# Two chained feed-forward layers behind a scan: the first two blocks of the first layer interleaved, with the weights loaded to match

## Chip, core and metric

One core of one Trainium2 chip. The metric is the device time of one execution in microseconds; the kernel before takes 623.9 us (median of three runs, 623.71 to 626.47).

## What is computed

A state-space scan over 4 sequences of 768 tokens (8 heads, 32 values and 16 states per head, chunks of 32 tokens), then two dense layers over the 3072 tokens, each 256 to 2048 to 256:

```python
for c in range(nc):                       # 24 chunks of 32 tokens
    M = CB * L                            # decayed C B^T inside the chunk
    y[:, :, sl] = einsum(M, xc) + einsum(Cc, state) * exp(cum)
    state = decay_full * state + sum(Bx)  # carried to the next chunk
x = attn_out.transpose(0, 2, 1, 3).reshape(B * S, H * D)
x = leaky_relu(x @ moe_w_in, 0.01) @ moe_w_out
return relu(x @ moe2_w_in) ** 2 @ moe2_w_out
```

## The kernel before

The tokens are cut into 12 **pieces** of 256. A piece is scanned in two halves. `scan_a` (lines 336 to 379) makes the scaled fp16 operands, the decays and the product S; `scan_b` (381 to 423) carries the states, forms Y on TensorE in two steps (lines 397 to 399, then 418 and 419) and ends with `yh` on ScalarE and `yl` on VectorE (lines 422 and 423). `yh` and `yl` are the input of the first layer, as a high and a low part; `yl` comes last, and no product of a block starts before it. From the second piece on, fp16 operands that are spread out over heads (`kbd`, `xbh`, `xbl`, `sbd`) are written by four DMAs each on the SP queue (line 332).

The first layer runs in **blocks**: six of one piece, then three of two. A block has 16 slices of the 2048 hidden values. In a one-piece block a step takes two slices: 12 matmuls for the hidden values (`hmm`, lines 443 to 445, into one of three PSUM buffers `hp`), two ScalarE instructions and one VectorE instruction that split the activation into `g` (lines 466 to 468), and, two steps later, 12 matmuls into the block's output `oo` (`omm`, lines 485, 486 and 491). So a block of one piece has 8 steps, 96 hidden matmuls and 96 output matmuls.

The weights lie in memory as 64-bit pairs. One **chunk** (512 KB) serves one step's hidden matmuls (`1i`) or output matmuls (`1o`). It is loaded by SP into one of seven staging buffers (`wst`), and takes three ScalarE (lines 126, 129, 161) and three VectorE instructions (137, 139, 162) to become two fp32r parts. The queue `wq` (line 105) holds all 8 chunks of `1i`, then all 8 of `1o`, then the second layer's. `w_step` works one chunk of each phase on; it is called once per step while chunks of the first layer remain.

The order of the program is fixed by the loop over blocks at line 643. `stages_to(due(...))` (lines 612 and 625) says how far the scans have come at each step; within a stage, `scan_b` of one piece and `scan_a` of the next are drawn in turn (line 601), except in stage 1, where `scan_b` runs first (line 597). Each engine takes its instructions in the order it was given, which a scheduler derives from the program's order and the dependencies. The second layer (`Two`, lines 509 to 582) follows when all blocks are done.

Of the kernel before, what the change touches and what calls it, by code (L numbers as in the profile page):

```python
# [24 lines left out]
NP = BATCH * NPC  # L25
# [5 lines left out]
KI, KO = DM // P, FF // P  # L31
# [6 lines left out]
LAG = {1: 2, 2: 3}  # L38
# [2 lines left out]
RATE = 1.4 / KO  # L41
LEAD = 4
NSTEP = 15
NHEAP = 24


# [5 lines left out]
def ssd_moe_kernel(ctx: ExitStack, tc: tile.TileContext, in1, in2, w1i, w1o, w2i, w2o, out):  # L52
# [10 lines left out]
    sm = ctx.enter_context(tc.tile_pool(name="sm", bufs=2))  # L63
    heap = ctx.enter_context(tc.tile_pool(name="heap", bufs=NHEAP))
    ap_ = ctx.enter_context(tc.tile_pool(name="ap", bufs=2))
# [5 lines left out]
    def big(shape, dtype, name, tag="b", bufs=None):  # L71
        return heap.tile(shape, dtype, tag=tag, name=name, bufs=bufs)
# [29 lines left out]
        return t[:, 0], t[:, 1]  # L102


    wq = [(nm, c) for nm in ("1i", "1o", "2i", "2o") for c in range(8)]
    w_loaded, w_half, w_full = [], [], []

    def load_w():
# [83 lines left out]
    def load_piece(p):  # L192
        v = sp.tile([P, U * (N + T + D)], F32, tag="in1", name="in1", bufs=2)
        w = sp.tile([P, U * 2 * T], F32, tag="in2", name="in2", bufs=2)
        nc.sync.dma_start(v, in1[p])
        nc.sync.dma_start(w, in2[p])
        return part(v, N + T, D), part(v, 0, N), part(w, T, T), part(v, N, T), part(w, 0, T), part(w, 0, T + N)
# [89 lines left out]
    def sequence_scales(s):  # L287

        mx = sm.tile([P, 5], F32, tag="mx", name="mx")
        all_ = in1[NPC * s : NPC * s + NPC].rearrange("a p f -> p a f")  # L290

        for to, at in ((0, N + T), (3, N + T + 16), (1, N), (4, N + 16), (2, 0)):
            t = big([P, NPC, U * 16], F32, "all", "st", 7)
            nc.sync.dma_start(t, all_[:, :, U * at : U * (at + 16)])
            yield
            squares(mx[:, to : to + 1], t)
            yield
        sc, isc, sbp = yield from powers(mx, 5)

        fac = sm.tile([P, 1], F32, tag="fac", name="fac")  # L300
        nc.vector.tensor_tensor(fac, isc[:, 0:1], isc[:, 2:3], ALU.mult)
        nc.vector.scalar_tensor_tensor(fac, fac, 1.0 / KK, isc[:, 1:2], ALU.mult, ALU.mult)
        for p in range(NPC * s, NPC * s + NPC):
            scales[p] = sc[:, 0:1], sc[:, 2:3], sc[:, 1:2], sbp, fac, KK, 1.0
# [121 lines left out]
    blocks, q0 = [], 0  # L426
# [75 lines left out]
    def split_y(g):  # L502
        y = yf.pop(g)
        h, l = (big([P, 2, KI, TP], F32R, t, "y", 4) for t in ("xh", "xl"))
        nc.scalar.copy(h, y)
        nc.vector.tensor_tensor(l, y, h.bitcast(F32), ALU.subtract)
        ys[g] = h, l
# [77 lines left out]
    def piece_y(p):  # L585
        return lambda: tuple(t[:, p % 2] for t in y_of(p))
# [6 lines left out]
    def stage(k):  # L593
        a = scan_a(k, loaded.pop(k)) if k < NP else iter(())
        b = scan_b(k - 1, piece_y(k - 1)) if k > 0 else iter(())
        bd = sequence_scales(k // NPC + 1) if k % NPC == NPC - 1 and k + 1 < NP else iter(())
        if k == 1:
            yield from b
        n = 0
        live = [b, a, bd]  # L600
        while live:
            live = [g for g in live if next(g, g) is not g]
            n += 1
            if n == 4 and k + 1 < NP:
                loaded[k + 1] = load_piece(k + 1)
            yield

    sc_it = (k for k in range(NP + 1) for _ in stage(k))
    now = [0, 0]
    cum = []  # L610

    def stages_to(x):
        while now[0] < NP + 1 and now[0] + min(now[1] / NSTEP, 0.99) < x:
            k = next(sc_it, NP + 1)
            now[:] = (k, now[1] + 1) if k == now[0] else (k, 0)

    stages_to(1)
    stages_to(1 + 13.5 / NSTEP)
    for _ in range(8):
        w_step()  # L620


    starts = [(KO * p0 - LEAD, p0 + n + 1) for p0, n in blocks[1:]]

    def due(at):
        return max(nb - max(RATE * (b - at), 0) for b, nb in starts)

    pend = []

    def second(lag):  # L630
        while len(pend) > lag:
            ph_, ms, end = pend.pop(0)
            ph_.omm(ms)
            if end:
                ph_.finish()

    def need(nm, m):
        while (nm, m) not in w_done:
            (w_step if nm[0] == "1" else w_one)()

    pos = 0
    acc = 0.0
    for i, (p0, n) in enumerate(blocks):
        ph_ = One(p0, n)
        for m in range(0, KO, 2 // n):
            ms = list(range(m, m + 2 // n))
            need("1i", m // 2)
            ph_.hmm(ms)
            pos += 2
            ph_.act(ms)  # L650
            stages_to(due(pos + 2))
            pend.append((ph_, ms, ms[-1] == KO - 1))
            if len(pend) > LAG[n]:
                need("1o", pend[0][1][-1] // 2)
            second(LAG[n])
            first_w = wq[:1] and wq[0][0][0] == "1" or any(v[0][0] == "1" for v in w_loaded + w_half + w_full)
            acc += 1.0 if first_w else (0.3 if i < len(blocks) - 1 else 1.5)
            while acc >= 1:
                acc -= 1
                (w_step if first_w else w_one)()  # L660
            if i == len(blocks) - 1 and m == KO - 4:
                split_y(0)
        if p0 % 2 + n == 2:
            ys.pop(p0 // 2)
    second(0)

    for g in range(NG):
        ph_ = Two(g)
# [64 lines left out]
```

## Time and profile before

| | |
|---|---|
| median of three runs | 623.9 us |
| profiled execution, its own time | 623.66 us |
| its span, first to last instruction | 621.9 us (1.76 us lie around it) |
| TensorE busy | 574.2 us (92%) |
| VectorE busy | 462.8 us (74%) |
| ScalarE busy | 450.8 us (72%) |

TensorE is busy in nine tenths or more of every slice of the span from about 90 us on, save the last; nearly all of its idle time lies ahead of that. VectorE and ScalarE are fullest in the first 60 us, where the scans of the first pieces and the weights of the first layer are worked on at once. Times below are counted from the start of the span.

### The profile page before, as it was taken

The page shows a single profiled execution, that of the slowest core. Times are in us where ns is not written, and L with a number is a line of the kernel's source. Part 1 is how long each engine was busy: PE and PEld are TensorE (multiplying, and loading weights), DVE is VectorE, ACT ScalarE, POOL GpSimd, SP SyncE. Part 2 cuts the span into 40 slices and gives each one's busy share as a digit, 9 for nine tenths or more (in the row PEclk, how much of TensorE's full clock was granted, in tenths as well). Part 3 has the DMA queues.
Part 4 walks back from the last instruction along what each step waited for, and adds up shares of the span by engine and source line. Part 5 has one row for each costly group of instructions (what it writes and reads, how often), then busy time and mean ns, then how long its engine had stood idle before and what let it go on. Part 6 is the DMA issues. An engine that isn't in the chain of part 4 may idle for free.

```text
span 621.9 us, 11809 instructions
## 1 busy us (share of the span) xinstructions
PE 574.2 (92%) x4674; PEld 521.6 (84%) x4674; DVE 462.8 (74%) x782; ACT 450.8 (72%) x723; POOL 5.2 (1%) x15
## 2 busy tenths in 40 slices
PE   0284889999999999999999999999999999999996
PEld 0274889899999978888888889989999999999996
DVE  6999799876688867645847457786787777777765
ACT  6996798766867765545666578877877878777773
POOL 3000000000000000000000000000000000000000
PEclk9985889999999999999999999999999999999999
DMA  8657766267357633202301000010010000100101
GB/s 322 211 130 225 231 184 156 28 155 236 47 110 199 185 65 53 28 10 52 87 24 35 0 2 2 0 35 1 1 34 1 9 27 1 35 1 1 35 1 35
DMA packets 113575, 46.52 MB, mean 75 GB/s; under 512 B 94448, under 2 KB 103280, under 8 KB 113520
## 3 DMA queue, kind: packets, MB, share of 16 engines
q1 hardware_dynamic: 113520, 45.76, 27.8%
q8 instruction: 37, 0.61, 0.4%
q14 instruction: 18, 0.15, 0.1%
HBM read 36.83 MB, written 3.15 MB: 64 GB/s over the span
## 4 chain that ended last, share of the span: by engine, by line
PE 83%; DVE 10%; ACT 3%; DMA 1%; issue 1%; DVEq 0%; ACTq 0%
PE hp L443 13%; PE hp L444 13%; PE hp L445 13%; PE o L485 4%; PE oo L485 4%; PE o L564 4%; PE o L491 4%; PE o L486 3%; PE o L562 3%; PE o L563 3%; PE oo L486 3%; PE oo L491 3%; PE Ym L564 3%; PE Ym L563 3%; PE Ym L562 3%
## 5 line engine op out<-in xcount | busy, mean ns | idle before, releaser
L443 PE MATMUL hp<-yl,w1i 128*128 128x256 f32 (+1 forms) x288 | 94.8, 329 | 9.1 <-DVE yl L423 6.4
L468 DVE TENSOR_TENSOR g<-t,g 128x512 fp32r<-128x512 f32 x96 | 65.7, 685 | 42.2 <-ACT t L467 39.7
L540 DVE TENSOR_TENSOR tl<-ts,th 128x1024 fp32r<-128x1024 f32 x48 | 58.8, 1225 | 49.2 <-ACT th L538 49.2
L445 PE MATMUL hp<-yh,w1i 128*128 128x256 f32 (+1 forms) x288 | 94.0, 326 | 0.0
L444 PE MATMUL hp<-yh,w1i 128*128 128x256 f32 (+1 forms) x288 | 93.8, 326 | 0.0
L466 ACT ACTIVATE g<-hp 128x512 fp32r<-128x512 f32 x96 | 57.2, 596 | 38.8 <-PE o L491 25.8
L528 ACT ACTIVATE b<-hp 128x512 f32<-128x512 f32 x96 | 57.2, 596 | 35.4 <-PE hp L445 35.4
L443 PE MATMUL hp<-xl,w2i 128*128 128x512 f32 x192 | 75.3, 392 | 0.0
L444 PE MATMUL hp<-xh,w2i 128*128 128x512 f32 x192 | 75.2, 392 | 0.0
L445 PE MATMUL hp<-xh,w2i 128*128 128x512 f32 x192 | 74.7, 389 | 0.0
L443 PEld LDWEIGHTS hp<-yl,w1i 128*128 128x128 f32 x288 | 56.8, 197 | 13.5 <-issue 4.0
L538 ACT CAST th<-ts 128x1024 fp32r<-128x1024 f32 x48 | 50.2, 1047 | 15.8 <-DVE ts L537 15.6
L445 PEld LDWEIGHTS hp<-yh,w1i 128*128 128x128 f32 x288 | 56.8, 197 | 3.7
L444 PEld LDWEIGHTS hp<-yh,w1i 128*128 128x128 f32 x288 | 56.8, 197 | 3.6
L485 PE MATMUL oo<-g,w1o 128*128 128x256 f32 x192 | 51.9, 300 | 8.3 <-DVE w1o L162 8.3
L467 ACT ACTIVATE t<-hp 128x512 f32<-128x512 f32 x96 | 57.3, 597 | 0.0
L529 ACT ACTIVATE b<-b 128x1024 f32<-128x1024 f32 x48 | 50.9, 1061 | 1.1
L486 PE MATMUL oo<-g,w1o 128*128 128x256 f32 x192 | 50.6, 293 | 0.0
L485 PEld LDWEIGHTS oo<-g,w1o 128*128 128x128 f32 x192 | 38.4, 200 | 9.1 <-DVE w1o L162 9.1
L539 DVE TENSOR_TENSOR bl<-b,bh 128x768 fp32r<-128x768 f32 x48 | 45.6, 951 | 0.0
L535 DVE TENSOR_TENSOR ts<-b 128x512 f32<-128x512 f32 x48 | 33.1, 690 | 13.4 <-ACT b L529 12.5
L445 PEld LDWEIGHTS hp<-xh,w2i 128*128 128x128 f32 x192 | 36.1, 188 | 7.9
(159 smaller groups left out, 1530.2 us busy)
## 6 DMA issues: line engine op xcount, KB each, us to landing
in<-in SPq DMA_DIRECT2D x12, 640.0 KB, 5.2
in<-in SPq DMA_DIRECT2D x12, 512.0 KB, 5.7
all<-in SPq DMA_DIRECT2D x15, 384.0 KB, 5.7
wst<-w1i SPq DMA_DIRECT2D x8, 512.0 KB, 8.4
wst<-w1o SPq DMA_DIRECT2D x8, 512.0 KB, 4.6
wst<-w2i SPq DMA_DIRECT2D x8, 512.0 KB, 6.8
wst<-w2o SPq DMA_DIRECT2D x8, 512.0 KB, 4.2
out_t<-r SPq DMA_DIRECT2D x24, 128.0 KB, 1.7
```

The lines of the kernel that those rows point to most:

```text
L443: nc.tensor.matmul(hp, wh[:, k, c], xl[:, :, k], start=(k == 0), stop=False)
L444: nc.tensor.matmul(hp, wh[:, k, c], xh[:, :, k], start=False, stop=False)
L445: nc.tensor.matmul(hp, wl[:, k, c], xh[:, :, k], start=False, stop=(k == KI - 1))
L466: nc.scalar.activation(g[:, 0], hp, AF.Lrelu)
L467: nc.scalar.activation(t, hp, AF.Lrelu)
L468: nc.vector.tensor_tensor(g[:, 1], t, g[:, 0].bitcast(F32), ALU.subtract)
L485: nc.tensor.matmul(self.o[d], wl[:, c], gh, start=(m == 0 and (d == 0 or self.n == 2)), stop=False, **kw)
L486: nc.tensor.matmul(self.o[d], wh[:, c], gh, start=False, stop=False, **kw)
L528: nc.scalar.activation(b[:, 2 * i : 2 * i + 2], hp.rearrange("p (n t) -> p n t", n=2), AF.Relu)
L529: nc.scalar.activation(b, b, AF.Square)
L538: nc.scalar.copy(th, t)
L540: nc.vector.tensor_tensor(tl, t, th.bitcast(F32), ALU.subtract)
```

## The change

The first two blocks are interleaved. The steps run: 6 steps of block 0, 6 steps of block 1, the last 2 of block 0, the last 2 of block 1; then block 2 as before. The weights follow: chunks 0 to 5 of `1i`, 0 to 5 of `1o`, 6 and 7 of `1i`, 6 and 7 of `1o`. In stages 1 to 3 `scan_b` of a piece runs ahead of `scan_a` of the next, and the pacing of these stages counts their steps accordingly. Every engine executes the same set of instructions as before; only their order differs, and from the middle of the kernel on the order is the same too.

```diff
+APART = 3
+FIRST = 12
...
-    wq = [(nm, c) for nm in ("1i", "1o", "2i", "2o") for c in range(8)]
+    wq = [(nm, c) for cs in (range(FIRST // 2), range(FIRST // 2, 8)) for nm in ("1i", "1o") for c in cs]
+    wq += [(nm, c) for nm in ("2i", "2o") for c in range(8)]
...
-        if k == 1:
+        if k <= APART:
             yield from b
...
-        while now[0] < NP + 1 and now[0] + min(now[1] / NSTEP, 0.99) < x:
+        while now[0] < NP + 1 and now[0] + min(now[1] / (2 * NSTEP if now[0] <= APART else NSTEP), 0.99) < x:
...
-    stages_to(1 + 13.5 / NSTEP)
+    stages_to(1.5)
...
-    starts = [(KO * p0 - LEAD, p0 + n + 1) for p0, n in blocks[1:]]
+    todo = []
+    for i, (p0, n) in enumerate(blocks):
+        todo += [(i, list(range(m, m + 2 // n))) for m in range(0, KO, 2 // n)]
+    k = FIRST // 2
+    todo[k:KO] = todo[KO // 2 : KO // 2 + k] + todo[k : KO // 2] + todo[KO // 2 + k : KO]
+    at_ = [2 * [i for i, _ in todo].index(i) for i in range(len(blocks))]
+    starts = [(at - LEAD, p0 + n + (0.5 if p0 + n <= APART else 1)) for at, (p0, n) in list(zip(at_, blocks))[1:]]
...
-    for i, (p0, n) in enumerate(blocks):
-        ph_ = One(p0, n)
-        for m in range(0, KO, 2 // n):
-            ms = list(range(m, m + 2 // n))
+    for i, ms in todo:
+        p0, n = blocks[i]
+        m = ms[0]
+        if i not in ones_:
+            ones_[i] = One(p0, n)
+        ph_ = ones_[i]
```

What this does to the engines' order is seen at three places. First VectorE around the `yl` that block 1 waits for (the second instruction that writes `yl_328`; numbers tell buffers apart). Before, these rows stand at 138 to 146 of its list:

```order
L468 TENSOR_TENSOR g_911<-t_910,g_911 128x512
L162 TENSOR_TENSOR w1o_927<-wst_431,w1o_927 128x512
L206 MEMSET in2_630 128x16
L468 TENSOR_TENSOR g_950<-t_949,g_950 128x512
L162 TENSOR_TENSOR w1o_966<-wst_657,w1o_966 128x512
L468 TENSOR_TENSOR g_989<-t_988,g_989 128x512
L392 SCALAR_TENSOR_TENSOR ql_1033<-le_625,sc_543,qh_1032 128x512
L423 SCALAR_TENSOR_TENSOR yl_328<-Y_573,fac_361,yh_327 128x512
L209 SCALAR_TENSOR_TENSOR le_1039<-in2_630,delta_89 128x512
```

In the changed kernel these stand at 126 to 134 (lines are three higher):

```order
L142 SCALAR_TENSOR_TENSOR wst_440<-wst_440 128x512
L165 TENSOR_TENSOR w1o_824<-wst_431,w1o_824 128x512
L140 SCALAR_TENSOR_TENSOR wst_587<-wst_587 128x512
L165 TENSOR_TENSOR w1o_863<-wst_440,w1o_863 128x512
L142 SCALAR_TENSOR_TENSOR wst_587<-wst_587 128x512
L354 SCALAR_TENSOR_TENSOR kmx_890<-in2_375,sc_692,him_716 128x512
L359 SCALAR_TENSOR_TENSOR cl_891<-in1_374,sc_692,ch_717 128x512
L426 SCALAR_TENSOR_TENSOR yl_328<-Y_528,fac_361,yh_327 128x512
L165 TENSOR_TENSOR w1i_916<-wst_587,w1i_916 128x512
```

The `yl` of piece 1 moves from row 145 to row 133; the `yl` of piece 0 stands at row 68 in both. Second, VectorE around the `yl` of piece 2, which block 2 waits for. Before, rows 203 to 209:

```order
L162 TENSOR_TENSOR w2i_3003<-wst_1012,w2i_3003 128x512
L468 TENSOR_TENSOR g_1471<-t_1470,g_1471 128x512
L137 SCALAR_TENSOR_TENSOR wst_1174<-wst_1174 128x512
L139 SCALAR_TENSOR_TENSOR wst_1174<-wst_1174 128x512
L392 SCALAR_TENSOR_TENSOR ql_1476<-le_1039,sc_856,qh_1475 128x512
L423 SCALAR_TENSOR_TENSOR yl_1342<-Y_1090,fac_563,yh_1341 128x512
L209 SCALAR_TENSOR_TENSOR le_1482<-in2_1141,delta_89 128x512
```

Now, rows 194 to 200:

```order
L140 SCALAR_TENSOR_TENSOR wst_1078<-wst_1078 128x512
L140 SCALAR_TENSOR_TENSOR wst_1171<-wst_1171 128x512
L165 TENSOR_TENSOR w2i_3104<-wst_1023,w2i_3104 128x512
L426 SCALAR_TENSOR_TENSOR yl_1266<-Y_1103,fac_712,yh_1265 128x512
L395 SCALAR_TENSOR_TENSOR ql_1473<-le_1276,sc_1044,qh_1472 128x512
L503 COPY yf_1503<-oo_733 128x256
L142 SCALAR_TENSOR_TENSOR wst_1078<-wst_1078 128x512
```

This `yl` moves from row 208 to row 197, so 64 rows lie behind the one of piece 1 where 63 did. Third, the SP queue near its start (`in1` and `in2` are the two inputs of a piece, `wst` a weight chunk). Before, rows 7 to 13:

```order
L195 DMA in1_162<-in1 128x1280
L196 DMA in2_163<-in2 128x1024
L117 DMA wst_371<-w1i 128x2x256
L117 DMA wst_377<-w1i 128x2x256
L117 DMA wst_386<-w1i 128x2x256
L195 DMA in1_456<-in1 128x1280
L117 DMA wst_395<-w1i 128x2x256
```

Now, rows 7 to 13:

```order
L198 DMA in1_162<-in1 128x1280
L199 DMA in2_163<-in2 128x1024
L198 DMA in1_374<-in1 128x1280
L120 DMA wst_380<-w1i 128x2x256
L199 DMA in2_375<-in2 128x1024
L120 DMA wst_386<-w1i 128x2x256
L120 DMA wst_395<-w1o 128x512
```

The first input of piece 2 moves ahead of the fifth chunk of `1i`, and the second input ahead of the sixth; the seventh load is now the first chunk of `1o`.

## Rows read from the trace of the kernel before

**Rows 1.** Busy time of each engine, granted clock (PEclk) and DMA, three stretches.
```profile
45.00:60.00 15.00, 7.57 (x86) 7.00 (x86) 14.82 (x35) 9.70 (x20) 0.00 (x0) 0.61 0.71 203
75.00:90.00 15.00, 13.22 (x127) 12.63 (x126) 13.48 (x27) 12.38 (x23) 0.00 (x0) 0.83 0.73 236
90.00:105.00 15.00, 15.00 (x152) 14.96 (x151) 14.66 (x28) 14.67 (x28) 0.00 (x0) 1.00 0.63 111
```

**Rows 2.** What TensorE waited for from 30 us on: total, times, longest.
```profile
PE oo L485 <- DVE w1o L162: 8.3, 3, 6.2
PE hp L443 <- DVE yl L423: 6.4, 3, 2.8
...
PE o L485 <- DVE yf L500: 0.8, 1, 0.8
```

**Rows 3.** TensorE in order of time: start, duration, line, operands, count, wait before.
```profile
50.51 0.21 PE L398 MATMUL Y<-mkl,xbh 128*128 128x48 f16 x1
50.55 0.21 PE L399 MATMUL Y<-mkh,xbl 128*128 128x48 f16 x1
...
57.53 0.41 PE L485 MATMUL oo<-g,w1o 128*128 128x256 f32 x1
57.75 0.41 PE L486 MATMUL oo<-g,w1o 128*128 128x256 f32 x1
...
73.87 0.55 PE L443 MATMUL hp<-yl,w1i 128*128 128x256 f32 x1 [2.12 <-DVE yl L423]
...
111.51 0.36 PE L443 MATMUL hp<-yl,w1i 128*128 128x256 f32 x1 [1.53 <-DVE yl L423]
111.70 0.28 PE L444 MATMUL hp<-yh,w1i 128*128 128x256 f32 x1
111.82 0.28 PE L445 MATMUL hp<-yh,w1i 128*128 128x256 f32 x1
```

**Rows 4.** VectorE in order of time, single instructions of the scans.
```profile
30.44 0.74 DVE L423 SCALAR_TENSOR_TENSOR yl<-Y,fac,yh 128x512 fp32r<-128x512 f32 x1
...
37.12 0.74 DVE L351 SCALAR_TENSOR_TENSOR kmx<-in,sc,him 128x512 f16<-128x512 f32 x1
...
38.45 1.22 DVE L214 TENSOR_TENSOR_SCAN le<-in,d1e 128x512 f32<-128x512 f32 x1
...
40.23 0.48 DVE L373 SCALAR_TENSOR_TENSOR in<-in,sc,le 128x256 f32<-128x256 f32 x1
40.62 0.68 DVE L370 TENSOR_TENSOR le<-in,le 128x512 f32<-128x512 f32 x1
41.22 0.17 DVE L204 TENSOR_SCALAR d1e<-in 128x16 f32<-128x16 f32 x1
...
47.80 0.93 DVE L389 TENSOR_TENSOR mkl<-in,mkh 128x768 f16<-128x768 f32 x1
...
72.98 0.74 DVE L423 SCALAR_TENSOR_TENSOR yl<-Y,fac,yh 128x512 fp32r<-128x512 f32 x1
...
110.62 0.75 DVE L423 SCALAR_TENSOR_TENSOR yl<-Y,fac,yh 128x512 fp32r<-128x512 f32 x1
```

**Rows 5.** VectorE's busy time between the three `yl`, and in block 2.
```profile
30.44:72.98 42.54, 39.39 (x78) 0.80 0.66 170
72.98:110.62 37.64, 34.63 (x64) 0.91 0.68 190
111.00:136.00 25.00, 20.16 (x32) 1.00 0.47 107
```

**Rows 6.** Loads of piece 2 and of `1i`: SP's issue, ScalarE's use, time to landing.
```profile
15.86 0.33 SPq L195 DMA_DIRECT2D in<-in  x1
...
24.86 0.65 ACT L126 ACTIVATE wst<-wst 128x512 f32<-128x512 f32 x1
...
wst<-w1i SPq DMA_DIRECT2D x8, 512.0 KB, 8.4
```

More of the change, by code (lines that the diff above doesn't have):

```diff
@@ L642, in ssd_moe_kernel @@
     acc = 0.0
-    for i, (p0, n) in enumerate(blocks):
-        ph_ = One(p0, n)
-        for m in range(0, KO, 2 // n):
-            ms = list(range(m, m + 2 // n))
[L647 to L663, printed above, removed]
+    ones_ = {}
+    for i, ms in todo:
[4 more added lines that the diff above has]
+        ph_ = ones_[i]
+        need("1i", m // 2)
+        ph_.hmm(ms)
+        pos += 2
+        ph_.act(ms)
+        stages_to(due(pos + 2))
+        pend.append((ph_, ms, ms[-1] == KO - 1))
+        if len(pend) > LAG[n]:
+            need("1o", pend[0][1][-1] // 2)
+        second(LAG[n])
+        first_w = wq[:1] and wq[0][0][0] == "1" or any(v[0][0] == "1" for v in w_loaded + w_half + w_full)
+        acc += 1.0 if first_w else (0.3 if i < len(blocks) - 1 else 1.5)
+        while acc >= 1:
+            acc -= 1
+            (w_step if first_w else w_one)()
+        if i == len(blocks) - 1 and m == KO - 4:
+            split_y(0)
+        if ms[-1] == KO - 1 and p0 % 2 + n == 2:
             ys.pop(p0 // 2)
```

## Prediction, made before the changed kernel ran

> **What bounds the kernel now.** I read the profile by stretches of time first. From 90 us on TensorE is busy all the time at the full clock (15.00 of 15.00 us, clock 1.00); ahead of that it is not: between 45 and 60 us it works 7.57 of 15 us at a mean clock of 0.61, while VectorE is busy 14.82 of 15 [rows 1]. ScalarE has room there (9.70). So the head is VectorE's, the rest TensorE's. The list of waits names what TensorE lacked: 8.3 us for split chunks of `1o`, 6.4 us for three `yl` [rows 2]. The last of these ends at 111.51, the first hidden product of block 2 [rows 3]; after it TensorE has one wait of 0.8 us until the end [rows 2]. Both blocks 0 and 1, hidden and output, are done by then in either kernel. So **the whole question is when block 2 starts**: the 510.4 us from there to the end of the span hold the same work, which TensorE does without pause, and a microsecond won or lost at that start is one of the total, unless the head leaves a debt that is collected later.
>
> **What VectorE has to do up to that start.** The three `yl` that open blocks 0, 1 and 2 start at 30.44, 72.98 and 110.62 [rows 4]; TensorE follows 0.89 us later (73.87 and 111.51) [rows 3]. VectorE is busy 39.39 of the 42.54 us between the first two and 34.63 of the 37.64 us between the second pair [rows 5], so I count its rows in the new order.
>
> Up to the first `yl` both kernels have 68 rows of the same kinds, some swapped. I leave 30.44 as it is.
>
> *From the first to the second.* Before 77 rows, now 65. The twelve that leave belong mostly to the first half of the scan of piece 2, which now comes behind. Durations overlap by 0.08 us: line 370 lasts 0.68, but the next row starts 0.60 later [rows 4]. By rows 4 less that overlap, the scan at line 214 costs 1.14, lines 361, 378 and 392 are of the form of `kmx` at 0.66 each, line 389 is 0.85, line 370 is 0.60, line 373 is 0.40; one `g` and one subtraction of a weight split are of line 370's form, 0.60 each; the three small rows of piece 3's decays (204 to 206) are about 0.4. Sum: 1.14 + 3 x 0.66 + 0.85 + 3 x 0.60 + 0.40 + 0.4 = 6.6 us. What stays is 39.4 - 6.6 = 32.8 us. Twelve chunks are still split ahead of this `yl`, but they feed six steps of two blocks rather than more of one, and the first output products no longer stand behind eight `1i` chunks and piece 2, which was the 6.2 us wait. Idle time is between 0 (VectorE never waits) and the 3.2 us of before. Those 3.2 came right ahead of `yl`, while TensorE finished output products that had waited for `1o`; now the second half of piece 1 stands behind 55 output products, with 17 behind it. I take 0.8, nearer to zero, because VectorE holds other work there. The second `yl` starts at 30.4 + 32.8 + 0.8 = 64.0 and block 1 at 64.9, where 73.87 stood.
>
> *From the second to the third.* Before 63 rows, now 64: two of line 139 leave (1.2) and one each of 351 and 356 (1.3); one of 162, 370, 373 and `g` come (2.2), and one scan (1.14). That is +0.8: 34.6 + 0.8 = 35.4 us. TensorE's own work between the starts of blocks 1 and 2 is 10 steps of 24 products, 240 x 0.12 (111.70 to 111.82) = 28.8 us, and 112 small products at no more than 0.04 (50.51 to 50.55), 4.5 us [rows 3]: 33.3 at the full clock, less than VectorE's 35.4 and close to it. Two engines that alternate so closely will wait for each other; the bounds are 0 and the 3.0 us of before. I take 1.2, below the middle, since TensorE is no longer stopped by `1o` chunks. The third `yl` starts at 64.0 + 36.6 = 100.6, block 2 at 101.5 rather than 111.51: **10.0 us earlier**.
>
> *Behind that start.* Eleven VectorE rows now stand between this `yl` and the first `g` of block 2, some 6.0 us by the same prices; TensorE has 36 hidden products and 32 small ones, 4.3 + 1.3 = 5.6 us, to cover them. I charge the difference, 0.4 us.
>
> *ScalarE and SP.* ScalarE executes what it did; it is busy 12.38 of 15 us in the stretch before the full one [rows 1], under VectorE, and the squares of piece 2 that stood ahead of the second step's activation move behind it. That frees a PSUM buffer sooner. I cost it at nothing; if it were as full as VectorE, its surplus would come on top. The four-part DMAs of `kbd`, `xbh`, `xbl` and `sbd` keep their order within a piece; `sbd` of piece 1 is queued behind loads whose buffers are free by then.
>
> [...]
>
> **The rivals.**
>
> *A, slower: the clock stays low between the starts of blocks 1 and 2.* Each of the 240 products then costs 0.09 us more. At 64.9 there are 46.6 us up to the old 111.51; 33.3 are needed at the full clock, so the change loses once more than (46.6 - 33.3) / 0.09 = 148 products run low. With all 240 low, block 2 starts at 64.9 + 33.3 + 21.6 = 119.8, 8.3 later: 632. For it: the 0.83 [rows 1]. Against it: work and time are nearly equal here (33.3 of 36.6 us), and at 90 to 105 us, where the trace of before shows TensorE full, the clock is 1.00. 5%.
>
> *B, the debt is collected.* The net 5.8 us that VectorE no longer does ahead of block 2 (6.6 - 0.8) must be done in it. VectorE was busy 20.16 of 25 us there [rows 5]; with 5.8 more it has 26. If TensorE waits for all of it, 5.4 us beyond my 0.4 are given back: 619.5. Against it: only `g` and the next `yl` have dates, the rest may slide into later blocks, which have room. 18%.
>
> *C, SP's queue.* Piece 2's first input cannot be issued before its buffer is free, at 15.86 [rows 6]; it now stands ahead of the fifth `1i` chunk, and the second input, which waits for the read at line 389, ahead of the sixth. ScalarE takes the fifth at 24.86; the median landing is 8.4 us, so it lands at some 16.2 + 8.4 = 24.6 [rows 6], just in time. Late by 3 to 5 us, it would stop ScalarE ahead of the first `yh`, and everything shifts: 617 to 619. [...] 8%.
>
> *D, no change.* The change moves the waits, not the sum: idle time of VectorE grows by what was taken out, since `oo` of both blocks and `hp` tie the engines together. 624. For it: of the 10.0 us only 5.8 are work taken out (39.4 + 34.6 = 74.0 us before, 32.8 + 35.4 = 68.2 now); the other 4.2 are idle time that I expect to shrink and that could double instead. 7%.
>
> **How the numbers follow.** The profiled execution took 623.66 us, 0.24 under the median; against its own time the sum is 623.66 - 10.0 + 0.4 = 614.1, and **614.2** for the median. Without any idle time block 2 would start 2.0 earlier and the 0.4 may vanish: 611.7; with TensorE's restart covered better still, 610.5. With all of the old idle time (3.2 + 3.0) it is 4.2 later: 618.4. My forecast is 610.5 to 617, 62%; B up to 619.5 comes to 18%, C lies in the same interval. The range is 610.5 to 619.5, which leaves out A, D and some of the tails. A measurement tells about 0.5% (3.1 us) from no change: under 620.8 is faster. That is the forecast, B and C: 0.88; D: 0.07; A: 0.05.
>
> **What would show it.** In the changed kernel the second `yl` on VectorE should start near 64 and the third near 100.6; the first hidden product of block 2 near 101.5, and TensorE without a wait over 1 us behind it. The 6.2 us wait for `1o` should be split and smaller. A `yl` at 66 or later with ScalarE idle at 20 to 28 us means C; a clock below 0.9 between 70 and 100 us means A; new waits of `oo` for `g` or of `hp` for `yl` beyond 101 us mean B. I am wrong if block 2 starts on time and the end does not follow.

## The result and the profile after

The changed kernel takes 616.6 us (median of four runs, 615.80 to 616.77) where the kernel before took 625.2 beside it on the same chip (623.71 to 626.47): a ratio of 0.9861, 95% interval 0.9830 to 0.9892. It is faster, 2.4 us above the forecast of 614.2 and inside the range. The profiled execution took 616.77 us with a span of 615.0 (621.9 before). Lines of this kernel are three higher than before.

VectorE in order of time (start, duration, line, operands, wait ahead), the three `yl` that open blocks 0, 1 and 2 and the rows just ahead of the third, to set against [rows 4]:

```profile
29.85 0.75 DVE L426 SCALAR_TENSOR_TENSOR yl<-Y,fac,yh 128x512 fp32r<-128x512 f32 x1
...
63.35 0.75 DVE L426 SCALAR_TENSOR_TENSOR yl<-Y,fac,yh 128x512 fp32r<-128x512 f32 x1 [0.42 <-ACT yh L425]
...
97.51 1.48 DVE L140 SCALAR_TENSOR_TENSOR wst<-wst 128x512 int32<-128x512 int32 x2
98.91 0.68 DVE L165 TENSOR_TENSOR w2i<-wst,w2i 128x512 fp32r<-128x512 f32 x1
99.51 0.74 DVE L426 SCALAR_TENSOR_TENSOR yl<-Y,fac,yh 128x512 fp32r<-128x512 f32 x1
```

The second and the third `yl` start at 63.35 and 99.51, where 72.98 and 110.62 stood. The rows ahead of the third split second-layer chunks, which are first used behind all nine blocks. TensorE, against [rows 3]:

```profile
65.28 0.28 PE L446 MATMUL hp<-yl,w1i 128*128 128x256 f32 x1
...
100.31 0.39 PE L446 MATMUL hp<-yl,w1i 128*128 128x256 f32 x1 [1.53 <-DVE yl L426]
...
101.68 0.42 PE L446 MATMUL hp<-yl,w1i 128*128 128x256 f32 x1
101.89 0.42 PE L447 MATMUL hp<-yh,w1i 128*128 128x256 f32 x1
...
104.89 0.36 PE L446 MATMUL hp<-yl,w1i 128*128 128x256 f32 x1
105.08 0.28 PE L447 MATMUL hp<-yh,w1i 128*128 128x256 f32 x1
105.20 0.28 PE L448 MATMUL hp<-yh,w1i 128*128 128x256 f32 x1
```

Block 1 starts at 65.28 without a wait, block 2 at 100.31, 11.2 us earlier than 111.51, after a wait of 1.53 us as before. But what follows differs: before, products came every 0.12 us at once [rows 3]; now, after two hidden products and 32 small ones, 16 products come every 0.21 us, from 101.46 to 104.89. The granted clock is 0.50 from 101.63 to 105.04, after 1.00 since 64.1. The waits from 30 us on (total, times, longest), against [rows 2], and the three stretches of [rows 1] (PE, PEld, DVE, ACT, POOL busy, then clock):

```profile
PE oo L488 <- DVE w1o L165: 6.2, 4, 4.2
PE hp L446 <- DVE yl L426: 3.8, 2, 2.2
PE S L311 <- ACT sq L256: 1.0, 2, 0.8
```

```profile
45.00:60.00 15.00, 8.73 (x93) 7.89 (x92) 15.00 (x38) 14.78 (x29) 0.00 (x0) 0.79 0.69 185
75.00:90.00 15.00, 14.83 (x160) 14.54 (x160) 14.85 (x29) 13.25 (x26) 0.00 (x0) 1.00 0.65 189
90.00:105.00 15.00, 13.24 (x145) 12.75 (x144) 14.75 (x31) 13.43 (x25) 0.00 (x0) 0.89 0.43 72
```

The worst of the head is still the stretch from 45 to 60 us: TensorE works 8.73 of 15 us, VectorE all of it, ScalarE 14.78 (9.70 before), and the longest wait for a split of `1o` is 4.2 us. A mark that has the same work behind it in every kernel is the first product of block 6, the first block of two pieces (512 columns). Before and after:

```profile
217.38 0.40 PE L443 MATMUL hp<-yl,w1i 128*128 128x512 f32 x1
```

```profile
210.42 0.40 PE L446 MATMUL hp<-yl,w1i 128*128 128x512 f32 x1
```

From there to the end of the span both take the same (404.5 and 404.6 us). So of the 11.2 us at block 2's start, 7.0 are left at block 6, and those reach the end.

### The profile page after: what moved, and what is told of

Same layout as the page of the kernel before. It is cut to its first block, busy times and chain, and to the rows that moved or that the text cites. A ratio compares the mean times of both kernels' runs of the same rounds, so it can differ in the third digit from the quotient of the medians.

```text
span 615.0 us, 11796 instructions
## 1 busy us (share of the span) xinstructions
PE 573.6 (93%) x4674; PEld 520.5 (85%) x4674; DVE 461.3 (75%) x782; ACT 450.4 (73%) x723; POOL 5.2 (1%) x15
## 4 chain that ended last, share of the span: by engine, by line
PE 77%; ACT 9%; DVE 9%; issue 2%; DMA 1%; SPq 0%; DVEq 0%; ACTq 0%
PE hp L446 13%; PE hp L447 13%; PE hp L448 13%; PE o L488 4%; PE o L567 4%; PE o L494 4%; PE o L489 4%; PE o L565 4%; PE o L566 3%; PE Ym L567 3%; PE Ym L566 3%; PE Ym L565 3%; PE oo L488 2%; PE oo L489 2%; PE oo L494 2%
## 5 line engine op out<-in xcount | busy, mean ns | idle before, releaser
L447 PEld LDWEIGHTS hp<-yh,w1i 128*128 128x128 f32 x288 | 56.9, 197 | 3.6
L488 PE MATMUL oo<-g,w1o 128*128 128x256 f32 x192 | 50.6, 293 | 6.2 <-DVE w1o L165 6.2
L489 PE MATMUL oo<-g,w1o 128*128 128x256 f32 x192 | 50.0, 291 | 0.0
```

What stands on the lines that cost most here:

```text
L447: nc.tensor.matmul(hp, wh[:, k, c], xh[:, :, k], start=False, stop=False)
L488: nc.tensor.matmul(self.o[d], wl[:, c], gh, start=(m == 0 and (d == 0 or self.n == 2)), stop=False, **kw)
L489: nc.tensor.matmul(self.o[d], wh[:, c], gh, start=False, stop=False, **kw)
```

## The experiments

"Before" below is the kernel before on the same chip. Ratios have their 95% interval. The theories, as the expectations name them: the start of block 2 is set by VectorE's rows ahead of the third `yl`; or the interleave matters, because TensorE no longer stops for `1o`; and the wait of 1.5 us itself lets the clock fall.

### One part of the change at a time

The scans' part (order and pacing) without the interleave:

```diff
-FIRST = 12
+FIRST = 16
```

> The changed kernel without the interleave: blocks 0 and 1 run one after the other and the weights load as before (all of 1i, then all of 1o); only the order of the scan halves in stages 1 to 3 and its pacing are the new ones. Theory V (the start of block 2 is set by what VectorE has ahead of the third yl): between the first and the third yl VectorE has 69.1 us of work here, 73 before, 67.1 with the whole change, so block 2 starts 3 to 5 us earlier than before and the time is 619 to 621 us. Theory W (the interleave matters because TensorE no longer waits for chunks of 1o): the wait of 6 us for w1o stays, nothing is won, 623 to 625 us.

Measured: 616.5 us (615.56 to 618.39), before 623.2, ratio 0.9883 (0.9852 to 0.9914). TensorE's waits for `w1o` are 1.4 us in all, without any interleave, and the third `yl` starts at 101.20, 9.4 us earlier than before. The interleave without the scans' part:

```diff
-APART = 3
+APART = 1
```

> The changed kernel with the scan halves drawn in turn as before in stages 2 and 3 (APART = 1), interleave and weight order kept. Theory V: VectorE has 72.0 us between the first and the third yl, only 1 less than before, so block 2 starts 1 to 3 us earlier: 621 to 623 us. Theory W: chunks of 1o come after six of 1i, TensorE's waits for them shrink as in the whole change, and most of the 8 us is won: 616 to 618 us.

Measured: 625.3 us (622.38 to 627.88), ratio 1.0036 (1.0014 to 1.0057): nothing won, a little lost. The second `yl` starts at 69.84, and TensorE waits 6.01 us for a `1o` split at 57.75, as before. (The profiled run took 622.38, the fastest of ten.) So **the gain is the scans'**, and the theory of the interleave has fallen. The count of VectorE's rows was too timid, however: by it 3.9 us of work had left (73 to 69.1) and 619 to 621 was expected, but the scans' part alone brings nearly all. Which rows stand ahead of the `1o` splits matters more than how many there are.

### Which line of the scans' part

One line, put into the kernel before (blocks, weights and pacing untouched):

```diff
-        if k == 1:
+        if k <= 3:
             yield from b
```

> The kernel before with one line of the change: scan_b ahead of scan_a in stages 1 to 3, pacing, blocks and weights as before. In VectorE's list the split of the first 1o chunk moves from row 121 to row 96, and the second yl from row 145 to row 133, as in the kernel with the whole of the scans' part. By the theory that what counts is which VectorE rows stand ahead of the first 1o splits and the second yl (the first half of piece 2's scan stood there): the 6.2 us wait for w1o at 57 us and the slow products behind it go, and the time is 616 to 618.5. By the theory that the pacing is needed (block 1's start still tied to a whole stage): 621 to 625.

Measured: **613.5 us** (613.25 to 615.71), before 624.3, ratio 0.9834 (0.9808 to 0.9860). That one line brings at least as much as the whole change: the changed kernel, on the same chip, took 616.2 (614.33 to 617.43; ratio 0.9858, 0.9829 to 0.9888). Its median is 2.7 us higher, but the two intervals overlap. One further run tells what the interleave does beside the line (against the changed kernel):

```diff
-APART = 3
+APART = 1
...
-        if k <= APART:
+        if k <= 3:
```

> The changed kernel without its pacing: blocks interleaved, weights in the new order, scan_b ahead of scan_a in stages 1 to 3, but pacing and the stages' end ahead of blocks 1 and 2 as in the kernel before. The third yl stands at row 186 of VectorE's list rather than 197. By the theory that the new pacing is what costs the changed kernel 2.7 us against the one line alone, and the interleave costs nothing: 612.5 to 614.5, with the third yl near 94 to 96 and no TensorE wait there. By the theory that the interleave itself costs (TensorE waits 4.2 us for the third 1o split at 55 us, which stands at row 101 of VectorE's list here too, and its next products are slow): 615 to 617.5. If the interleave brings something of its own: 610 to 612.

Measured: 617.0 us (615.50 to 617.26), before 623.7, ratio 0.9886 (0.9866 to 0.9906), above that of the line alone, and the two intervals do not touch. The third `yl` comes at 93.72, earlier than with the line alone (95.51), and it helps nothing. The reason stands on VectorE between 46 and 62 us. Before, in order of time:

```profile
46.67 1.21 DVE L209 TENSOR_TENSOR_SCAN le<-in,delta 128x512 f32<-128x512 f32 x1
...
48.72 1.22 DVE L214 TENSOR_TENSOR_SCAN le<-in,d1e 128x512 f32<-128x512 f32 x1
...
55.02 0.74 DVE L361 SCALAR_TENSOR_TENSOR xl<-in,sc,xh 128x512 f16<-128x512 f32 x1
...
56.20 0.68 DVE L162 TENSOR_TENSOR w1o<-wst,w1o 128x512 fp32r<-128x512 f32 x1
```

With the one line:

```profile
48.56 0.69 DVE L162 TENSOR_TENSOR w1o<-wst,w1o 128x512 fp32r<-128x512 f32 x1
...
52.62 0.67 DVE L162 TENSOR_TENSOR w1o<-wst,w1o 128x512 fp32r<-128x512 f32 x1
...
56.17 0.69 DVE L162 TENSOR_TENSOR w1o<-wst,w1o 128x512 fp32r<-128x512 f32 x1
...
58.68 1.22 DVE L209 TENSOR_TENSOR_SCAN le<-in,delta 128x512 f32<-128x512 f32 x1
```

With the one line and the interleave:

```profile
48.88 0.67 DVE L165 TENSOR_TENSOR w1o<-wst,w1o 128x512 fp32r<-128x512 f32 x1
...
49.61 1.22 DVE L212 TENSOR_TENSOR_SCAN le<-in,delta 128x512 f32<-128x512 f32 x1
...
56.20 0.68 DVE L373 TENSOR_TENSOR le<-in,le 128x512 f32<-128x512 f32 x1
...
60.27 0.69 DVE L165 TENSOR_TENSOR w1o<-wst,w1o 128x512 fp32r<-128x512 f32 x1
```

Before, most of the first half of the scan of piece 2 (from line 209 to line 373) stood ahead of the first `1o` split of block 0, which ended at 56.9; TensorE waited 6.17 us for it. With the one line that split starts at 48.56 and the scan follows behind the fourth. With the interleave besides, the scan lies between the third split (48.88) and the fourth (60.27), and TensorE's wait comes back, the longest of all kernels here:

```profile
61.01 0.58 PE L488 MATMUL oo<-g,w1o 128*128 128x256 f32 x1 [9.53 <-DVE w1o L165]
```

The new pacing then repairs part of this (4.2 us in the changed kernel instead of 9.53). Line and pacing 0.9883, line and interleave 0.9886, all three 0.9858, the line alone 0.9834: in the medians each of the other two parts costs something. Only the interval of line and interleave lies clear of that of the line alone.

### The clock behind a wait

Twelve further products of 256 columns ahead of block 2, which need only `yh` and write where the block's first product starts afresh, so that TensorE works while `yl` is made:

```diff
+            if self.p0 == 2 and ms[0] == 0:
+                for _ in range(FILL):
+                    nc.tensor.matmul(self.h[:, 0:n], w_of("1i", 0)[0][:, 0, 0:P], self.x[0][:, :, 0], start=True, stop=True)
```

> The changed kernel with 12 extra matmuls of 256 columns (their result is overwritten) that need only yh of piece 2, so that they run in TensorE's wait for yl ahead of block 2. They cost nothing if they fit in that wait of 1.5 us. Theory C (the wait itself lets the clock fall, and the products of block 2 that run at 0.21 us each until about 105 us cost 1.7 us): the clock stays at 1.00 and the time is 1 to 2 us lower than the changed kernel, 614.5 to 615.5 us. Rival (the clock falls for another reason, or the extra matmuls delay block 2): the clock is low between 100 and 105 us as it was, 616.5 to 618 us.

> The changed kernel once more, on the chip of the next run and timed beside it: 616 to 617.5, and in the profile a clock under 1.00 for some microseconds behind the wait for the third yl, if that wait is 1.5 us as before.

> The changed kernel with twelve further products of 256 columns ahead of block 2, on yh of piece 2 and into a buffer that the block's first product overwrites, so that TensorE works while it waits for the third yl. By the theory that the wait of 1.5 us itself lets the clock fall and costs 1.7 us: 1.5 to 2 us under the changed kernel of the same call, 614.5 to 615.5. By the rival that the clock behind that start varies from run to run whatever TensorE did: within 0.5 us of it, or slower by the fillers' own 1.4 us.

Measured: at first 615.4 us (613.70 to 617.22; ratio 0.9862, 0.9830 to 0.9895); then 614.9 (614.20 to 615.71; ratio 0.9850) beside 616.2 of the changed kernel. Each run has its mean granted clock, and sorted by it the times fall roughly into line:

| kernel | us at clock, each run |
|---|---|
| changed (both sets of runs) | 617.43, 616.77, 616.77, 616.68, 616.38 at 0.988; 616.23 at 0.990; 615.80 at 0.991; 614.33 at 0.992; 614.50 at 0.993 |
| with filler (both sets) | 617.22 at 0.988; 615.72 at 0.989; 615.00 at 0.992; 615.71 at 0.993; 615.01, 614.88 at 0.994; 614.20, 613.70 at 0.997 |
| one line | 615.71 at 0.988; 613.75, 613.49 at 0.992; 613.38, 613.25 at 0.995 |
| interleave only | 627.88 at 0.974 to 622.38 at 0.991, ten runs |

By the medians of the second set the filler is 1.3 us faster, a little under the 1.5 to 2 of the theory, but the intervals overlap (0.9824 to 0.9877 against 0.9829 to 0.9888). Its profiled run there has a clock of 1.00 from 90 to 105 us where the changed kernel's has 0.92. The fillers do not fill the whole wait: they need `yh`, and 1.02 us of waiting for it (1.06 in the first set) are left ahead of them. At one and the same clock it is no gain (615.71 against 614.50 at 0.993, one run each; it adds work), so what it wins it wins by the clock. But the clock varies from run to run whatever precedes it, as the rival has it: two of eight filler runs fell as low as the changed kernel. It differs even ahead of the fillers, where TensorE, VectorE and ScalarE have the same order in all three profiles. From 50 to 70 us the clock is 0.74 in the second profile of the changed kernel, 0.83 and 0.91 in the two with the filler, and the third `yl`, which no filler can move, starts at 99.98, 99.07 and 97.88. And the kernel with the interleave alone waits longer at this very place, 3.21 us, and goes on at 0.12 us a product:

```profile
108.97 0.36 PE L446 MATMUL hp<-yl,w1i 128*128 128x256 f32 x1 [3.21 <-DVE yl L426]
109.17 0.28 PE L447 MATMUL hp<-yh,w1i 128*128 128x256 f32 x1
109.29 0.28 PE L448 MATMUL hp<-yh,w1i 128*128 128x256 f32 x1
```

That the idle wait lets the clock fall is not shown, then; why it fell here stays open.

### Second-layer chunks out of the way

The rows of second-layer splits ahead of the third `yl` can go later. In the changed kernel:

```diff
-    wq += [(nm, c) for nm in ("2i", "2o") for c in range(8)]
+    later = [(nm, c) for nm in ("2i", "2o") for c in range(8)]
...
+        if at == HOLD:        # 18
+            wq.extend(later)
...
-        acc += 1.0 if first_w else (0.3 if i < len(blocks) - 1 else 1.5)
+        acc += 1.0 if first_w else (0.5 if i < len(blocks) - 1 else 1.5)
```

> The changed kernel with the weights of the second layer queued only from the third step of block 2 on (and split faster afterwards, 0.5 steps instead of 0.3), so that VectorE has 60.1 us of work between the first and the third yl rather than 67.1. Theory V with C: TensorE becomes the bound between the starts of blocks 1 and 2, block 2 starts 1 to 2 us earlier, the wait ahead of it is under 0.5 us and the clock does not fall: 612.5 to 614.5 us. Rival (a debt: the second layer's weights are then late, or their work collides with block 2 and 3): new waits of TensorE behind 110 us, 616 us or more.

Measured: 613.2 us (612.95 to 613.29), before 623.2, ratio 0.9826 (0.9802 to 0.9851). The third `yl` starts at 93.44 instead of 99.51, and from 60 us on TensorE's longest wait is 1.28 us. The debt was not collected: block 6 starts at 206.12, 405.0 us from the end. Without the interleave (`FIRST = 16`):

> The scans' new order and pacing, blocks and first-layer weights in the old order (no interleave), and the second layer's chunks only from step 18 on, at 0.5 a step. By the theory that VectorE's rows alone decide and the interleave adds nothing: the third yl near 93 to 96, the time 612.5 to 615, level with the interleaved kernel that holds the second layer back (613.2). By the theory that the interleave is worth something as soon as VectorE is relieved, because TensorE then has products of block 1 where it waited for 1o: 615 to 617, with waits for w1o or for the second yl longer by 2 to 4 us in sum than in the interleaved one.

Measured: 613.6 us (612.99 to 613.80), before 624.5, ratio 0.9825 (0.9794 to 0.9856), with the third `yl` at 92.26: level, so the interleave adds nothing here either. In the kernel before, the same edit:

> The kernel before, with one edit: the chunks of the second layer are queued only from the first step of piece 3's block on (step 18 counting two slices as one), and at 0.5 a step then rather than 0.3. No change of the blocks' order or of the scans' order. By the theory that VectorE's rows ahead of the third yl set the start of block 2: the rows between the first and the third yl cost about 61.5 us by count rather than 73, but those taken out lie behind the second yl, which stays near 73. From 73.9 on TensorE is then the bound with its 33.3 us of products, so block 2 starts near 107 to 108 and the time is 619 to 621. By the theory that the second layer's chunks are harmless ahead of block 2 (they only fill VectorE's idle time): no change, 622 to 625. If they were the whole matter, whatever the scans' order: 613 to 615.

Measured: **no gain**: 627.4 us (621.44 to 629.90), before 624.5, ratio 1.0033 (1.0004 to 1.0062). The profiled run took 623.99, the second fastest of ten, and it is the most telling of all; no profile shows the eight slower runs (mean clock 0.974 to 0.979, here 0.985). The third `yl`:

```profile
99.74 0.75 DVE L425 SCALAR_TENSOR_TENSOR yl<-Y,fac,yh 128x512 fp32r<-128x512 f32 x1
```

It comes 10.9 us earlier than before. On TensorE, block 2 then starts at 105.91 and block 6 at 214.50:

```profile
105.91 0.28 PE L445 MATMUL hp<-yl,w1i 128*128 128x256 f32 x1
...
214.50 0.40 PE L445 MATMUL hp<-yl,w1i 128*128 128x512 f32 x1
...
228.20 0.77 PE L487 MATMUL o<-g,w1o 128*128 128x512 f32 x1 [2.46 <-DVE yf L502]
228.76 0.63 PE L488 MATMUL o<-g,w1o 128*128 128x512 f32 x1
...
230.04 0.63 PE L445 MATMUL hp<-yl,w1i 128*128 128x512 f32 x1
```

Block 2 is 5.6 us earlier, but 24 output products of block 1 that used to stand ahead of its start are now behind it, and at block 6 only 2.9 us are left. Those are given back at 228 us: TensorE waits 2.46 us for a copy (0.8 before, [rows 2]) and goes on with 0.43 us a product instead of 0.23. The copy, on VectorE, is late because ScalarE stood still for a second-layer chunk and VectorE then for ScalarE's part of its split (3.01 us; 2.88 before). ScalarE here and in the kernel before:

```profile
222.44 0.67 ACT L128 ACTIVATE wst<-wst 128x512 f32<-128x512 f32 x1 [2.47 <-DMA wst<-w2o]
```

```profile
222.64 0.68 ACT L126 ACTIVATE wst<-wst 128x512 f32<-128x512 f32 x1 [2.58 <-DMA wst<-w2o]
```

ScalarE goes on only 0.2 us earlier than before, and the copy starts 1.2 us earlier (227.64; 228.85 before). TensorE gets there 2.9 us earlier, so it waits 1.7 us longer. Expected were 4 us of gain; the step that failed is that an earlier block 2 is an earlier end. Two more combinations:

> The changed kernel with the second layer held back (as above), and the switch between blocks 0 and 1 after 4 steps instead of 6 (chunks 0 to 3 of 1i and 1o first, then 4 to 7). By the theory that VectorE's rows ahead of the second yl decide when block 1 can start: these are no fewer by count (61.0 us from the start of the kernel against 58.7), so the second yl comes at 63 to 66 and TensorE, which has two steps less to do ahead of it, waits 2 to 4 us more for it: 614 to 617. By the theory that what counts is how few chunks TensorE needs per product: w1o waits shrink from 6 us to 2 to 4 and the time is 610 to 612.

Measured (`FIRST = 8`): 622.2 us (619.61 to 624.03), ratio 0.9963 (0.9943 to 0.9983). Both theories' ranges are missed. That an earlier switch costs is right, its size is not: TensorE waits 4.6 us for the second `yl`, 7.3 us for an `sbd` DMA at 60 us that nobody had thought of, and 3.0 us for the copy of block 6.

> As one_line_order, with the second layer's chunks queued only from step 18 on and at 0.5 a step then. By the theory that the two causes add where the first one is out of the way (VectorE's rows ahead of the second yl by the order of the scans, those ahead of the third by the second layer's chunks): 612.5 to 615, 2 to 4 us under one_line_order. By the theory that holding back costs what it wins (as it did with the scans' old order, where ScalarE waited for a second-layer chunk at 222 us and TensorE 2.5 us for yf): within 1 us of one_line_order.

Measured (the one line and the later second layer): 615.6 us (614.86 to 616.39), ratio 0.9861 (0.9835 to 0.9888), 2.1 above the one line alone, so that both theories' ranges are missed; the two intervals overlap. The third `yl` comes earlier (93.19 against 95.51) and TensorE works less from 60 to 90 us (24.4 us against 26.7). Why its waits there grow was not followed up. The two remedies do not add here. Three kernels end level at 613.2 to 613.6, each faster than the changed kernel in its median: the one line alone, and the scans' part with the second layer held back, with the interleave and without it. The simplest is the one line.

## Why the prediction was right, and where it was not

**VectorE's rows up to the third `yl`: right.** The second `yl` was forecast at 64.0 and came at 63.35, the segment 33.6 us long in the sum and 33.50 in the trace; the third at 100.6, and came at 99.51, 36.6 against 36.16. VectorE is busy 32.77 and 35.11 us of the two segments (32.8 and 35.4 forecast) and idle 0.7 and 1.1 us (0.8 and 1.2). The rows were counted well. The idle times were choices between wide bounds, so their fit is in part luck.

**Block 2's start: 10.0 us earlier forecast, 11.2 measured.** Here TensorE still waits 1.53 us. Of the 1.2 us beyond the forecast 0.6 are the first `yl`, which was left at 30.44 and came at 29.85. No run shows the 1.2 us for TensorE's restart that lead from 611.7 to 610.5 in the range; block 2 began 0.80 us after the third `yl` did, 0.89 before.

**What lies behind that start: the term that was mis-sized.** 0.4 us were charged; 4.3 were given back, 4.2 of them between the starts of blocks 2 and 6 (105.9 us before, 110.1 after). Of these 1.5 are the 16 products at 0.21 rather than 0.12 us (the 101.46 to 104.89 stretch), 0.8 and 0.5 are two new waits (at 206.40 for ScalarE's `sq`, the third of the waits above, and at 129.65 for the next `yl`), and 0.8 is 32 small products of the scans, from 100.65 to 101.46, which stood ahead of block 2's start before and stand behind it now; 0.6 is not accounted for. The prediction took the 510.4 us behind block 2's start for the same work in both kernels. It was not, and the clock was not in the term at all. In the sum: 623.66 - 11.2 + 4.3 = 616.8, the profiled run (616.77). The forecast of 614.2 came as near as it did because two errors have opposite signs, 1.2 us at the start and 3.9 us behind it.

**"The whole question is when block 2 starts": wrong as a rule.** It held here since the waits ahead of it were removed with it. The kernel before with the second layer held back brought the `yl` 10.9 us forward and ended as late. What counts is TensorE's lost time: its waits, and the stretches in which it worked at the lower clock. From 30 us on, in each profiled run (waits added up; low clock is the time at a granted clock of 0.50, from the first product of block 0 to 240 us):

| kernel | third `yl` | waits, us | low clock, us | span, us |
|---|---|---|---|---|
| changed, second layer later | 93.44 | 11.9 | 10.2 | 611.1 |
| scans' part, second layer later | 92.26 | 12.6 | 3.4 | 611.2 |
| one line | 95.51 | 13.1 | 6.8 | 611.7 |
| one line, second layer later | 93.19 | 14.2 | 6.8 | 613.6 |
| interleave and one line | 93.72 | 16.9 | 13.7 | 614.9 |
| changed | 99.51 | 13.1 | 13.7 | 615.0 |
| scans' part | 101.20 | 14.7 | 13.7 | 616.6 |
| interleave only | 108.08 | 20.7 | 10.2 | 620.6 |
| before | 110.62 | 19.5 | 23.9 | 621.9 |
| changed, `FIRST = 8`, second layer later | 96.98 | 22.4 | 20.5 | 622.1 |
| before, second layer later | 99.74 | 21.2 | 17.1 | 622.2 |

The spans follow the two columns of lost time, roughly (a wait inside a low stretch counts in both), and not the date of the third `yl`. (An estimate from 0.21 and 0.12 us a product: while TensorE works, a microsecond at the lower clock loses some 0.4.) The changed kernel itself won 6.4 us of waits and 10.2 us of low clock.

**ScalarE: costed at nothing.** From 45 to 60 us it became as full as VectorE, 14.78 of 15 us. That shows as 0.42 us of VectorE's wait ahead of the second `yl`, so the term was small.

**Whose gain it was: not asked for.** The prediction priced the order of the scans and the interleave as one. It put the 6.2 us wait for `1o` down to eight `1i` chunks and piece 2 together. It was piece 2: with the interleave alone, where `1o` comes after six `1i` chunks, 6.7 us of waiting for `w1o` stay; with the scans' part alone 1.4 us are left, with the one line 0.4, and with the interleave besides 6.2 (in the changed kernel) to 10.0.

**The rivals.** A, the clock low between blocks 1 and 2: not seen, 1.00 from 64.1 to 101.6 us. The 0.09 us a product that it charges are the spacings of [rows 3], 0.21 from 57.53 on less 0.12 from 111.70 on. On either side of that stretch the clock was 0.50: from 53.8 to 64.1 us, where TensorE worked 7.16 of 10.24 us around waits of 4.22 and 1.29 us, and from 101.6 to 105.0 us, at a price of 1.5 us, although ahead of it TensorE had worked 35.6 of 37.5 us at 1.00, and its longest wait was 1.53 us. What lets it fall is not shown. B, the debt: no product of block 2 waited for `g`, and its 5.4 us did not come; the 4.3 us above are of another kind, but for the wait of 0.5 us for a `yl`. C, SP's queue: piece 2's load went out at 15.70 and the fifth `1i` chunk right behind it, at 16.07, as the rival has it; ScalarE took that chunk at 24.79 without a wait, and the first `yl` starts 0.6 us earlier than before, not later. D, no change: refuted by the interval.

## What to carry to other kernels

When an engine that feeds the bound is full, look for rows in its list that stand ahead of what the bound waits for and have a later date themselves; here moving that one group was worth at least the whole of a larger reordering, so time the parts alone. Judge a reordering at a mark that has the same work behind it in both kernels, not at the start of a block, and count the time at the lower clock (0.50 in these profiles) with the waits. A transfer that lands no earlier can take back what was won ahead of it: in the old order with the second layer held back, ScalarE went on 0.2 us earlier behind a load, and 2.9 us at block 6 were gone at the end.

## What the runs showed of the hardware

At one place, among the first output products of block 6, the kernels wait for the same copy, between 0.79 and 2.99 us. After 0.79, 0.82, 1.28 and 1.50 us (before, changed, second layer later, one line) the next hidden products came every 0.23 us; after 1.60 (the scans' part alone), 1.78 (interleave and one line), 2.46 (before, second layer later) and 2.99 us (`FIRST = 8`, second layer later) every 0.43 us for a while; but after 1.59 us (the filler, first set) and 1.89 us (interleave only) every 0.23. At block 2's start a wait of 1.53 us was followed by 0.12 us a product before and, 1.2 us later, by 0.21 in the changed kernel, and one of 3.21 us (interleave only) by 0.12. The length of the wait alone does not tell. The scans' part alone at that place, where the first four hidden products are 0.39 to 0.43 us apart and the next ones 0.23:

```profile
222.52 0.75 PE L488 MATMUL o<-g,w1o 128*128 128x512 f32 x1 [1.60 <-DVE yf L503]
...
225.20 0.63 PE L448 MATMUL hp<-yh,w1i 128*128 128x512 f32 x1
225.63 0.55 PE L446 MATMUL hp<-yl,w1i 128*128 128x512 f32 x1
226.02 0.39 PE L447 MATMUL hp<-yh,w1i 128*128 128x512 f32 x1
```

And one and the same program runs at different mean clocks from run to run, 0.974 to 0.991 for the interleave alone, whose times spread over 5.5 us with them. The changed kernel with the second layer later spreads over 0.34 us in four runs, at 0.989 to 0.991.
